# Gated linear attention and a channel mix on one core: gates taken two units ahead, masks placed per chunk, a new written order

## Chip, core and metric
One NeuronCore of a Trainium2 chip. The metric is device microseconds of one launch; lower is better. The profiled execution is one more launch, of which the profiler gives the span from the first to the last instruction.

## What is computed
Attention over 4 batches, 8 heads, 768 steps, head width 48, then a channel mix over 384 columns (mu_r and w_r are drawn eight times as large):

```python
f = 1.0 / (1.0 + np.exp(-f_logit))
for t in range(S):
    state = f[:, :, t, :, None] * state + np.einsum('bhd,bhe->bhde', k[:, :, t], v[:, :, t])
    y[:, :, t] = np.einsum('bhd,bhde->bhe', q[:, :, t], state)
x = y.transpose(0, 2, 1, 3).reshape(B, S, H * D)
x_prev = np.concatenate([zeros, x[:, :-1]], axis=1)
xk = mu_k * x + (1.0 - mu_k) * x_prev
xr = mu_r * x + (1.0 - mu_r) * x_prev
k = np.maximum(xk @ w_k, 0.0)
out = 1 / (1 + np.exp(-(xr @ w_r))) * (k * k @ w_v)
```

## The kernel before
**Tiling.** Time is cut into 24 chunks of 128 steps (six a batch); three chunks make a unit of 384 steps, eight units (u = 0 to 7) in all. Every unit passes through attention, chunk by chunk, and then through the mix.

**Attention, chunk i.** `b` is the running product of the gates (a DVE scan into PSUM), `bl` its last column; `ln` and `rb` on ACT give its reciprocal; `q`, `n`, `kr`, `k` scale the transposed queries and keys (DVE; `kr` on POOL). On PE, `TR` transposes k (4 matmuls), `S` forms the scores (32), `P` the chunk's sum of k and v (32), `YA` and `YB` the outputs (16 and 48). `kt` copies the transpose, `m` masks the scores, `zb`, `T`, `g`, `za` carry the state, `w` is a small copy between YA and YB, `y` writes the unit's input x, and three pairs of transfers `sp` spread two heads' rows over partitions (lines 189 to 365).

**Mix, unit u.** `d` and `xm` form the mixed inputs (0: for w_k, 1: for w_r), `xh` and `xl` split each into a high part in fp32r and the rest. `F` (8 blocks of 9 matmuls), `R` (3 of 9) and `W` (3 pairs of 12) multiply high x high, high x low and low x high. After F: `r` is the ReLU, `h` its square's high part, `kk` the square, `l` the square's low part. After R: `lg` is a copy and `sg` the sigmoid on ACT with its table load, and a load of the Exp table behind it. `o` is the product, `out` the store (lines 419 to 559).

**Weights** come as 64-bit words: 8 pieces of w_k, 4 of w_r, 6 of w_v. Each piece is loaded (`wk0`), turned into fp32 by three DVE steps (`wkS0`, `wkT0`, `wkX0`), and split by `wkH0` (ACT) and `wkL0` (POOL or DVE) (lines 561 to 603). `c` and `cm` load weights once more and reduce them for a range check; `lo`, `lot`, `lom`, `strong` turn that and the gates' least product into a flag, on which a general path (not taken here) hangs.

**Gates.** `f{u}` loads a unit's gate logits into one of three buffers. `sf{u}` is their sigmoid: units 0 to 2 have their own (line 387), and for unit 2 the Exp table is loaded behind it (line 389); unit u+3's is taken inside `sg{u}` (line 532).

**What sets the order.** Every instruction stands in one list written by hand, `ORDER` (lines 48 to 116); each engine's queue, SP's transfers among them, runs its words in the list's order and waits where data or a buffer isn't ready (lines 139 to 159, 700 to 713). A word's `/V`, `/A`, `/G` names the engine (DVE, ACT, POOL) where a task has a choice. A task's `after` list, its buffers and the list `chain` bound what an order may do: before, `chain` makes every F, R and W follow the one before it. PSUM gives four buffers `pm` that scans, transposes, weight steps and mix products share.

## Time and profile before
| | |
|---|---|
| median of 3 runs | 348.4 us (347.81 to 350.14) |
| the profiled execution's own time | 350.27 us |
| its span | 348.4 us |
| mean granted clock of TensorE | 0.981 |
| PE, DVE, ACT, POOL busy | 310.7, 253.7, 205.3, 168.0 us |
| transfers | 45.3 MB, 130 GB/s on the mean |

Busy time is the time in which an engine had an instruction in work; matmuls are pipelined, so a busy PE is not PE at its peak. A releaser (`<-`) is what ended an idle time. SPq is the queue that issues the transfers.

### The profile page before, as it was taken

To read this page: it belongs to the slowest core of one execution; us is meant where nothing else is said; L and a number is where in the kernel's file an instruction comes from. 1 tells how busy PE (TensorE), PEld (TensorE's weight loads), DVE (VectorE), ACT (ScalarE), POOL (GpSimd) and SP (SyncE) were. 2 spreads that over 40 slices of the span, in tenths; PEclk is the share of its full clock that TensorE was granted. 3 is DMA by queue.
4 is the path that set the end of the run, shared out by engine and by line. 5 is a ranking of instruction groups with operands and counts; after the bars stand their busy time and mean duration, and the time that the engine had idled before them with its cause. 6 is when DMAs were issued, how large, how long until landed. Compare 5 with 4: busy or idle time off the path is not lost.

```text
span 348.4 us, 10719 instructions
## 1 busy us (share of the span) xinstructions
PE 310.7 (89%) x4410; PEld 296.7 (85%) x4410; DVE 253.7 (73%) x521; ACT 205.3 (59%) x431; POOL 168.0 (48%) x209
## 2 busy tenths in 40 slices
...
GB/s 228 383 390 98 149 336 145 198 105 221 179 129 213 87 123 3 134 220 140 178 87 116 230 189 253 86 83 24 193 8 35 47 24 15 5 45 24 2 24 53
DMA packets 20649, 45.31 MB, mean 130 GB/s; under 512 B 2928, under 2 KB 13040, under 8 KB 20592
## 3 DMA queue, kind: packets, MB, share of 16 engines
...
q8 instruction: 36, 0.59, 0.7%
...
## 4 chain that ended last, share of the span: by engine, by line
PE 65%; DVE 15%; DMA 6%; issue 5%; ACT 3%; SPq 2%; POOL 2%; DVEq 0%; ACTq 0%; POOLq 0%
PE pm L468 55%; PE py L329 5%; DMA qk<-in_qkt 2%; PE pss L296 2%; DMA x<-stage 2%; PE pm L281 2%; DMA words<-in_wv 2%; DVE pm L590 1%; PE pss L316 1%; POOL k2l L505 1%; DVE pm L581 1%; DVE xm L445 1%; DVE pm L211 1%; DVE pm L428 1%; SPq L199 1%
## 5 line engine op out<-in xcount | busy, mean ns | idle before, releaser
L468 PE MATMUL pm<-xh,wk 128*128 128x384 f32 x384 | 105.7, 343 | 1.3 <-DVE words_k2l L593 0.6
L468 PE MATMUL pm<-wv,k2h 128*128 128x384 f32 x384 | 98.9, 339 | 0.8 <-DVE xm L445 0.8
L505 POOL TENSOR_TENSOR k2l<-kk,k2h 128x384 fp32r<-128x384 f32 x57 | 59.2, 1049 | 43.6 <-ACT k2h L495 25.6
L460 POOL TENSOR_TENSOR xl<-xm,xh 128x384 fp32r<-128x384 f32 x42 | 45.9, 1103 | 65.4 <-ACT xh L453 43.9
L468 PEld LDWEIGHTS pm<-xh,wk 128*128 128x128 f32 x384 | 70.0, 187 | 3.2 <-DVE words_k2l L593 0.8
L468 PEld LDWEIGHTS pm<-wv,k2h 128*128 128x128 f32 x384 | 68.7, 188 | 1.4 <-DVE xm L445 1.0
L468 PE MATMUL pm<-xl,wk 128*128 128x384 f32 x192 | 64.6, 337 | 0.0
L468 PE MATMUL pm<-wv,k2l 128*128 128x384 f32 x192 | 64.5, 336 | 0.0
L490 ACT ACTIVATE r<-pm 128x384 f32<-128x384 f32 x53 | 25.9, 491 | 32.2 <-PE pm L468 31.9
L468 PE MATMUL pm<-wr,xh 128*128 128x384 f32 x144 | 37.5, 341 | 1.9 <-DVE words L593 1.7
L211 DVE TENSOR_TENSOR_SCAN pm<-f,low 128x512 f32<-128x512 f32 x24 | 33.0, 1375 | 6.0 <-ACT ktk L285 3.7
L495 ACT ACTIVATE k2h<-r 128x384 fp32r<-128x384 f32 x64 | 32.8, 522 | 6.0 <-DVE r L491 4.6
L468 PEld LDWEIGHTS pm<-wv,k2l 128*128 128x128 f32 x192 | 36.1, 188 | 0.0
L468 PEld LDWEIGHTS pm<-xl,wk 128*128 128x128 f32 x192 | 36.1, 188 | 0.0
L497 DVE SCALAR_TENSOR_TENSOR kk<-pm,r 128x384 f32<-128x384 f32 x33 | 18.2, 555 | 19.3 <-ACT r L490 16.3
L555 DVE TENSOR_TENSOR o<-pm,lg 128x384 f32<-128x384 f32 x24 | 13.2, 551 | 24.6 <-PE pm L468 24.6
L281 PE MATMUL pm<-ident,qk 128*128 128x128 f32 x96 | 16.1, 294 | 16.2 <-DMA words_k2h<-in_wk 16.2
L229 POOL TENSOR_TENSOR qk<-qk,rb 128x256 f32<-128x256 f32 x21 | 16.3, 775 | 29.3 <-ACT bl L214 16.1
L329 PE MATMUL py<-qk,z 64*64 64x64 f32 x704 | 22.8, 235 | 8.4 <-ACT pm L437 7.0
L329 PEld LDWEIGHTS py<-qk,z 64*64 64x64 f32 x704 | 16.8, 140 | 14.8 <-ACT pm L437 7.2
L468 PEld LDWEIGHTS pm<-wr,xh 128*128 128x128 f32 x144 | 25.5, 188 | 2.6 <-DVE words L593 2.0
L281 PEld LDWEIGHTS pm<-ident,qk 128*128 128x128 f32 x96 | 12.2, 149 | 17.2 <-DVE qk L237 16.2
...
## 6 DMA issues: line engine op xcount, KB each, us to landing
...
```

Of the source, the lines that this page charges most:

```text
L211: pl.add(f"b{i}", ("V", lambda: nc.vector.tensor_tensor_scan(b().rearrange(FL), f().rearrange(FL), self.low.rearrange(FL), 1.0, op0=ALU.mu ...
L229: e.tensor_tensor(k()[:, ::2], k()[:, ::2], rb()[:, ::2], op=ALU.mult)
L281: nc.tensor.transpose(pk()[:, j], k()[:, j], self.ident)
L296: nc.tensor.matmul(self.pss[HALF[h], r, 64 * j : 64 * j + 64], k()[HALF[r], j, HALF[h]], q()[HALF[r], j, HALF[h ^ j % 2]], start=True, sto ...
L329: first[c, h] = nc.tensor.matmul(to, lhs, rhs, start=(c, h) not in first, stop=stop, skip_group_check=True)
L460: e.tensor_tensor(lo(), xm(), hi().bitcast(F32), op=ALU.subtract)
L468: nc.tensor.matmul(ps, lhs(a, j), rhs(bb, j), start=ends[0] and i == 0, stop=ends[1] and i == len(pr) - 1)
L490: pl.add(f"r{u}.{f}", ("A", lambda r=r, ps=ps: nc.scalar.activation(r(), ps(), AF.Relu)), ("V", lambda r=r, ps=ps: nc.vector.tensor_scalar ...
L495: pl.add(f"h{u}.{f}", ("A", lambda r=r, hi=hi: nc.scalar.activation(hi(), r(), AF.Square)), after=[f"r{u}.{f}"], **kw)
L497: pl.add(f"kk{u}.{f}", ("V", lambda r=r, ps=ps, kk=kk: nc.vector.scalar_tensor_tensor(kk(), ps(), 0.0, r(), op0=ALU.max, op1=ALU.mult)), ( ...
L505: e.tensor_tensor(lo(), kk(), hi().bitcast(F32), op=ALU.subtract)
L555: pl.add(f"o{u}.{t}", ("V", lambda t=t, ps=ps, o=o: nc.vector.tensor_tensor(o(), ps(), lg()[:, t], op=ALU.mult)), after=[f"W{u}.{t}1", f"s ...
```

## The change
- `AHEAD = 2`: the gates of unit u+2 (was u+3) are taken inside `sg{u}`; only units 0 and 1 have a sigmoid of their own. `b` of unit 2's chunks (6 to 8) now waits for `sg0`.
- The mask of every chunk is either one DVE step (`m/V`) or a copy by ACT (`m/A`) with a product on POOL (`mg/G`). Before, only chunk 0 had the second form; the new order gives it to chunks 0 to 5, 10, 13 to 18 and 20.
- `chain` is gone: F, R and W blocks of a unit may stand in any order, and among other units'.
- The mix's code is cut into functions (`add_inputs`, `add_square`) that could take a unit in parts; every unit is one part here, so names gain a 0 after the point (F0.02 is block 2 of unit 0) and sizes stay.
- `ORDER` is written anew. Parts moved between engines, before and after, as counts of words: `l` on POOL 57, 36, on DVE 7, 28; `xl` on POOL 42, 29, on DVE 6, 19; `za` on POOL 16, 10, on DVE 4, 10; `r` on DVE 11, 22; `kk` on DVE 33, 22; `xh` on DVE 23, 18; `lg` on DVE 4, 8.

```diff
@@ -28,8 +28,8 @@
 SIGMOID_SET = "sigmoid_and_others"
 EXP_SET = "natural_log_exp_and_others"
 LOW = 1.0e-18
-N, U = B * NCH, B * NU
-NQ, NFB = 4, 3
+N = B * NCH
+NQ, NFB, AHEAD = 4, 3, 2
 
 BUFS = {
     "pm": (4, [512]), "rb": (2, [NP, C]), "ss": (2, [2, NP, C // 2]), "ktk": (2, [NP, 2, D]), "v": (3, [H, D]),
@@ -41,78 +41,86 @@
 }
 
 
-AWAY = 1
-HALVED = 1
+UNITS = ((3,),) * (B * NU)
+FIRST = [sum(map(sum, UNITS[:u])) for u in range(len(UNITS) + 1)]
+U, FU = len(UNITS), N // UC
+HALVED = {0}
 
 
 ORDER = """
-f0.0 sf0.0 b0 bl0/V f0.1 sf0.1 b1 f0.2 sf0.2 f1 b2 wr0 wrS0 mu wrT0 wrX0 qk0 sf1 onemu b3 ex ln0 rb0 kr0/G q0 n0 bl1/A
-g2 ln1 qk1 q1 qk3 rb1 kr1/G q3 n1 ln3 rb3 bl3/A qk2 ln2 rb2 k0 cst k1 g1 n3 q2 kr3/G k3 TR0 S0 v0 kt0/A P0 TR1 bl2/A
-n2 m0 zb0/A wk0 wkS0 b4 YA0 w0/A kr2/G k2 S1 mg0 YB0 wkT0 ln4 kt1/A T0 za1/G g3 y0/A v1 m1 wkX0 P1 wk2 wr1 v2 TR2 wkS2
-rb4 kt2/A wv0 zb1 b5 T1 wvS0 wkT2 x00 YA1 wkH0 wrH0 bl4/A w1/A ln5 YB1 y1/A P2 wvT0 wkX2 wkH2 wv1 za2/G wrL0/G S2
-wkL2/G wkL0/G TR3 wvX0 kt3/A zb2 YA2 m2 S3 w2/A YB2 rb5 wrS1 wk6 wkS6 wrT1 wr2 f2 wkT6 wrX1 T2 za3/G wkX6 wvS1 wrS2
-qk4 kr4/G wvH0 wvL0/G wvT1 wrT2 v3 P3 y2/A qk5 kr5/G q4 wrX2 wvX1 sf2 wvH1 wvL1/G n4 m3 k4 g4 sp0.2 sp0.0 d0.00 xm0.00
-d0.12 zb3 YA3 d0.02 xm0.12 xm0.02 bl5/A xh0.00/A wk1 sp0.1 d0.01 wrH1 w3/A xh0.02/A S4 TR4 YB3 xl0.00/G wrL1/G xm0.01
-xl0.02/G xh0.01/A kt4/A wrH2 xl0.01/G wkS1 wk3 wkS3 d0.10 wkT1 wkT3 wkX1 wkH1 wkX3 wkH3 wkL1/G wkL3/G wrL2/G wk4 wk5
-wk7 wkS4 T3 wkT4 xm0.10 F0.0 wkH6 wkX4 y3/A x01 wkL6/G q5 n5 d0.11 xm0.11 k5 F0.1 wkS7 v5 r0.0/A kk0.0/A wv3 v6 v4 wr3
-h0.0 l0.0/G wkH4 r0.1/A kk0.1/A wkL4/G za4/G g5 wkS5 h0.1 l0.1/G F0.2 r0.2/A h0.2 wkT7 wv2 qk6 kk0.2/A l0.2/G wkT5
-wkX7 F0.3 r0.3/A wkX5 wkH5 wkL5/G wvS3 wrS3 wvT3 kk0.3/A h0.3 l0.3/G wkH7 xh0.10/A xl0.10/G P4 zb4 wvX3 wrT3 T4 za5/G
-wrX3 F0.4 r0.4/A TR5 YA4 xh0.11/A kk0.4/A kt5/A wvH3 F0.5 w4/A h0.4 m4 wrH3 wvS2 wkL7/V r0.5/A b6 wrL3/V xh0.12/A wvT2
...
-l7.5/G r7.6/A h7.6 kk7.6/V l7.6/G r7.7/A h7.7 kk7.7/V l7.7/G R7.0 R7.1 lg7.0/A R7.2 W7.00 W7.01 W7.10 W7.11 lg7.1/A
-lg7.2/A sg7 o7.0 out7.0 o7.1 W7.20 out7.1 W7.21 o7.2 out7.2
+wv0 f0.1 f0.0 f0.2 f1 wv1 qk1 qk0 qk2 wvS0 mu wvT0 v0 sf0.0 wvX0 sf0.1 cst b0 sf0.2 b1 wvH0 bl0/A sf1 b2 g1 wvS1 ex
+wvT1 bl1/A wvL0/V ln0 v1 ln1 wvX1 rb0 q1 wv2 rb1 kr0/G q0 n0 wk0 g2 k0 ln2 kr1/G qk3 bl2/A wk6 rb2 n1 S0 v2 q2 kr2/G
+wk4 TR0 k1 wk2 m0/A wvH1 n2 S1 kt0/A b3 wvL1/G P0 onemu wvS2 ln3 mg0/G TR1 zb0/A k2 m1/A YA0 wvT2 mg1/G kt1/A T0 w0/A
+wvX2 bl3/A rb3 YB0 za1/G q3 wvH2 kr3/G P1 qk4 wkS0 y0/A TR2 c7 zb1 wkS6 S2 g3 wkT0 wvL2/G YA1 m2/A n3 kt2/A wkT6 mg2/G
+wv3 T1 wkS4 wkX0 wkX6 w1/A b4 YB1 wkH6 wkL6/G P2 qk5 wkT4 bl4/A ln4 v3 k3 za2/G wk5 rb4 wkS2 wk7 y1/A kr4/G wkX4 zb2
+q4 wkH4 YA2 b5 w2/A YB2 T2 ln5 wkT2 wvS3 rb5 wkX2 kr5/G y2/A n4 TR3 q5 wkH2 za3/G S3 sp0.00 k4 bl5/A kt3/A g4 x00
+wkL4/G wvT3 wk1 TR4 n5 m3/A sp0.01 wkL2/G wkH0 wvX3 S4 kt4/A sp0.02 wkS5 wvH3 P3 cm7 d0.000 v4 wvL3/G wkT5 v5 d0.010
+c4 xm0.000 wk3 zb3 mg3/G xh0.000/A k5 wr2 YA3 m4/A c11 wkX5 TR5 d0.002 xl0.000/G xm0.010 d0.001 S5 xm0.002 w3/A wkH5
+wkL0/G xm0.001 xh0.002/A YB3 wkS1 xh0.001/A T3 d0.012 xl0.001/G xl0.002/V kt5/A za4/V P4 mg4/G y3/A wkT1 F0.02 zb4
+wkX1 xh0.010/A g5 cm4 wkL5/G m5/A xm0.012 wv5 F0.00 r0.02/A wr3 T4 mg5/G wkS3 kk0.02/A v6 wr0 d0.011 wrS2 wr1 YA4
+za5/G wkH1 wkT3 r0.00/A w4/V wkL1/G wkX3 YB4 kk0.00/A wrT2 wkH3 cm11 P5 xl0.010/G F0.04 y4/A zb5 c0 wrX2 f2 wkL3/G
+xm0.011 wrH2 f3 wvS5 xh0.011/A YA5 wrL2/G h0.00 wkS7 F0.05 w5/A xh0.012/A l0.00/G wkT7 h0.02 wvT5 r0.04/A l0.02/G YB5
+wvX5 kk0.04/A r0.05/A wkX7 F0.06 x01 xl0.011/G kk0.05/A wrS0 wkH7 wrT0 h0.04 xl0.012/G wrS1 wvH5 wrX0 F0.01 wrT1 y5/A
+wkL7/G wrX1 wrS3 wvL5/G wrH0 wrT3 F0.07 sp1.00 r0.01/A l0.04/V h0.05 wrX3 sp1.02 wrH1 wrL0/G r0.06/V wrH3 F0.03 wrL1/V
+kk0.01/A l0.05/G sp1.01 h0.01 wrL3/V h0.06 l0.01/G wv4 cm0 R0.0 qk8 r0.03/A qk6 kk0.06/A kk0.03/V c9 h0.03 l0.06/G
+d1.00 v7 r0.07/A R0.1 l0.03/G lg0.0/V kk0.07/A xm1.010 h0.07 R0.2 xm1.000 l0.07/G wvS4 xh1.000/A lg0.1/A wvT4 W0.20
+lg0.2/A d1.02 wvX4 xh1.010/V wvH4 d1.01 W0.10 sg0 wvL4/G xm1.011 xm1.002 xh1.002/V xl1.010/G c8 qk7 W0.11 xl1.000/G
+xm1.012 cm9 xl1.002/V c6 xm1.001 v8 W0.21 sf2 xh1.001/A b6 xl1.001/G W0.00 o0.1 ln6 b7 out0.1 rb6 bl6/V o0.2 ln7 W0.01
...
+kk6.05/A YB22 P23 y22/A F6.01 h6.05 R6.2 r6.01/A lg6.0/A kk6.01/V h6.06 zb23 h6.01 F6.07 lg6.2/A l6.01/G YA23 r6.07/V
+R6.1 w23/A kk6.06/V h6.07 m23/V l6.06/G cm10 lg6.1/A l6.05/G lo mg23/V YB23 kk6.07/A W6.00 sg6 y23/V l6.07/V sp7.00
+W6.01 sp7.02 sp7.01 d7.00 W6.10 xm7.010 xm7.000 xh7.010/A xh7.000/A xl7.010/G d7.01 W6.11 xl7.000/G o6.0 xm7.001
+out6.0 d7.02 xh7.001/A W6.20 xm7.012 xl7.001/G xm7.002 xh7.002/A xl7.002/G W6.21 F7.04 o6.2 o6.1 xm7.011 out6.1 F7.00
+r7.04/A xh7.011/V xl7.011/V F7.01 r7.00/V kk7.00/A h7.04 F7.07 h7.00 xh7.012/A l7.00/V kk7.04/A xl7.012/V l7.04/G
+F7.03 r7.07/A r7.01/A kk7.07/V h7.07 h7.01 F7.02 l7.07/G kk7.01/A F7.06 r7.02/A kk7.02/V R7.0 r7.06/A h7.02 l7.02/G
+F7.05 lg7.0/V r7.03/V kk7.03/A R7.1 h7.03 l7.03/G r7.05/V l7.01/V h7.05 R7.2 kk7.05/A h7.06 l7.05/G W7.10 lg7.2/A
+kk7.06/A lg7.1/A l7.06/G sg7 W7.00 W7.01 W7.11 o7.0 out7.0 out6.2 W7.20 o7.1 out7.1 lot W7.21 lom strong o7.2 out7.2
 """
...
-        if i < AWAY:
-            pl.add(f"m{i}", ("A", lambda: nc.scalar.copy(ss(), s4(self.pss[:, :, :256]))), after=I("S"),
-                   takes=[("ss", i)])
-            pl.add(f"mg{i}", ("G", lambda: nc.gpsimd.tensor_tensor(ss(), ss(), mask(), op=ALU.mult)),
-                   after=I("m"), uses=[("ss", i)])
-        else:
-            pl.add(f"m{i}", ("V", lambda: nc.vector.tensor_tensor(
-                ss(), s4(self.pss[:, :, :256]), mask(), op=ALU.mult)), after=I("S"), takes=[("ss", i)])
+        def masked():
+            nc.vector.tensor_tensor(ss(), s4(self.pss[:, :, :256]), mask(), op=ALU.mult)
+
+        pl.add(f"m{i}", ("V", masked), ("A", lambda: nc.scalar.copy(ss(), s4(self.pss[:, :, :256]))), after=I("S"),
+               takes=[("ss", i)])
+        pl.add(f"mg{i}", ("V", lambda: None), ("G", lambda: nc.gpsimd.tensor_tensor(ss(), ss(), mask(), op=ALU.mult)),
+               after=I("m"), uses=[("ss", i)])
...
+    def add_gates(self, pl, u):
...
-            if u < NFB:
-                def sf():
-                    nc.scalar.activation(t(), t(), AF.Sigmoid)
-                    if u == 2:
-                        nc.scalar.preload_act_table_set(EXP_SET)
-
-                pl.add(f"sf{u}", ("A", sf),
-                       after=[f"f{u}", "ex" if u > 1 else "sf0.2"])
+            if u < AHEAD:
+                pl.add(f"sf{u}", ("A", lambda: nc.scalar.activation(t(), t(), AF.Sigmoid)), after=[f"f{u}", "sf0.2"])
             else:
-                pl.add(f"sf{u}", ("A", lambda: None), after=[f"sg{u - NFB}"])
+                pl.add(f"sf{u}", ("A", lambda: None), after=[f"sg{self.turn(u)}"])
+
+    def turn(self, u):
+
+        return max(n for n in range(U) if FIRST[n] < UC * (u - AHEAD + 1))
...
-        chain = [f"W{u - 1}.{UC - 1}1"] if u > 0 and not alone else []
...
-            pl.add(f"F{u}.{f}", ("P", ff), after=chain + [f"xl{u}.0{j}" for j in range(KJ)]
-                   + ([] if alone else [f"wkL{f}"]),
-                   takes=[("pm", ("f", u, f))], uses=[("xh0", u), ("xl0", u)])
-            chain = [f"F{u}.{f}"]
...
-        more = not alone and u + NFB < U
+                   after=[f"R{u}.{t}"], **kw)
+        more = None if alone else next((w for w in range(AHEAD, FU) if self.turn(w) == u), None)
 
         def sig():
-            nc.scalar.activation(lg(), lg(), AF.Sigmoid)
+            nc.scalar.activation(lg()[:, :tiles], lg()[:, :tiles], AF.Sigmoid)
             if more:
-                t = self.f_t[u % NFB]
+                t = self.f_t[more % NFB]
                 nc.scalar.activation(t, t, AF.Sigmoid)
             if not alone and u < U - 1:
                 nc.scalar.preload_act_table_set(EXP_SET)
 
         pl.add(f"sg{u}", ("A", sig),
-               after=[f"lg{u}.{t}" for t in range(UC)] + ([f"f{u + NFB}"] if more else []) + (["ex"] if not alone else []),
+               after=[f"lg{u}.{t}" for t in range(tiles)] + ([f"f{more}"] if more else []) + (["ex"] if not alone else []),
                uses=[("lg", u)])
-        for t in range(UC):
+        for t in range(tiles):
             ps = lambda t=t: pm("v", u, t)[:, :DM]
...
                 pl.add(f"W{u}.{t}{h}", ("P", vp),
-                       after=chain + [f"l{u}.{f}" for f in range(NF // 2 * h, NF // 2 * (h + 1))]
+                       after=[f"l{u}.{of[t]}{f}" for f in range(NF // 2 * h, NF // 2 * (h + 1))] + [f"W{u}.{t}0"] * h
                        + ([] if alone else [f"wvL{p}" for p in range(3 * h, 3 * h + 3)]),
                        uses=[(f"k2h{h}", u), (f"k2l{h}", u)] + ([("pm", ("v", u, t))] if h else []),
                        takes=[] if h else [("pm", ("v", u, t))])
-                chain = [f"W{u}.{t}{h}"]
...
+    def add_inputs(self, pl, u, p, c, n, alone, halved):
+        nc = self.nc
+        x = lambda: self.b("x", u)
+        now, past = lambda j: x()[:, j, 1 + c : 1 + c + n], lambda j: x()[:, j, c : c + n]
+        xs = [] if alone else [("x", u)]
+        pm = lambda *key: self.b("pm", key)[:, :n]
+        own = lambda j: [] if alone else [f"sp{u}.{p}{j}"]
+        before = lambda j: [] if alone else [f"sp{u}.{p - 1}{j}" if p else f"x0{u}"]
...
+    def add_square(self, pl, u, f, p, c, n, mm3, alone):
+        nc = self.nc
+        h, fh = divmod(f, NF // 2)
+        key = (u, p, f)
+        name = f"{u}.{p}{f}"
+        ps = lambda: self.b("pm", ("f", *key))[:, :n]
+        xs = lambda a: self.b(("xh0", "xl0")[a], u)
+        ff = lambda: mm3(ps(), lambda a, j: self.w["wk"][a][:, j, f * P : f * P + P], lambda a, j: xs(a)[:, j, c : c + n],
+                         range(KJ))
+        pl.add(f"F{name}", ("P", ff), after=[f"xl{u}.{p}0{j}" for j in range(KJ)] + ([] if alone else [f"wkL{f}"]),
+               takes=[("pm", ("f", *key))], uses=[("xh0", u), ("xl0", u)])
...
```

## Rows read from the trace of the kernel before

**Rows 1.** Stretches of the profiled execution: its bounds and length in us, then busy time and instructions of PE, PE's weight loads, DVE, ACT and POOL, the granted clock, the DMA engines' share and GB/s; the last row sums all stretches.
```profile
10.00:20.00 10.00, 3.82 (x74) 3.07 (x74) 9.91 (x24) 7.82 (x16) 6.15 (x11) 1.00 1.05 374
20.00:30.00 10.00, 7.42 (x276) 6.07 (x276) 10.00 (x22) 7.28 (x23) 5.00 (x7) 1.00 0.87 329
30.00:40.00 10.00, 2.78 (x101) 2.62 (x100) 7.39 (x17) 6.64 (x10) 5.73 (x9) 0.75 0.14 37
40.00:50.00 10.00, 7.72 (x119) 6.81 (x120) 9.54 (x20) 9.31 (x25) 8.93 (x11) 0.74 0.92 293
50.00:60.00 10.00, 10.00 (x188) 9.10 (x187) 10.00 (x21) 9.39 (x23) 9.93 (x13) 1.00 0.53 214
60.00:70.00 10.00, 8.33 (x166) 7.73 (x165) 9.83 (x18) 7.52 (x20) 7.92 (x9) 1.00 0.59 179
...
120.00:130.00 10.00, 9.17 (x111) 9.02 (x100) 9.79 (x22) 3.42 (x8) 4.07 (x6) 1.00 0.51 156
...
170.00:180.00 10.00, 9.48 (x215) 8.76 (x213) 7.21 (x15) 6.75 (x18) 4.81 (x6) 1.00 0.52 186
...
sum 350.00, PE 310.73 PEld 296.69 DVE 253.71 ACT 205.33 POOL 168.03; mean PE 8.88 PEld 8.48 DVE 7.25 ACT 5.87 POOL 4.80
```
**Rows 2.** The chain of work that ended last, in order of time: start in us, length, what, and the count of merged instructions. L316 is P, L281 TR, L329 YA (x16) and YB (x48), L296 S, L468 the mix.
```profile
225.45 0.36 PE pss L316 x32
...
283.75 0.44 PE pm L281 x4
284.19 0.39 PE py L329 x16
284.58 0.47 PE pss L296 x32
285.05 0.72 PE py L329 x48
...
290.73 51.93 PE pm L468 x297
```
**Rows 3.** Instructions in order of time, PE at R0.0: start, length, engine, line, operation, output and inputs, count, and the idle time before it with what ended it.
```profile
64.50 0.62 PE L468 MATMUL pm<-wr,xh 128*128 128x384 f32 x2 [1.67 <-DVE words L593]
```
**Rows 4.** The same view, from 32 to 42 us: ACT at the sigmoid of load 2, and what DVE and PE waited for.
```profile
35.01 1.28 ACT L387 ACT_TABLE_LOAD   x1
36.31 1.48 ACT L387 ACTIVATE f<-f 128x1536 f32<-128x1536 f32 x1
37.81 1.28 ACT L389 ACT_TABLE_LOAD   x1
...
32.37 0.36 DVE L273 TENSOR_TENSOR sm<-pss,z 128x192 f32<-128x192 f32 x1 [1.20 <-PE pss L296]
40.27 0.61 DVE L440 SCALAR_TENSOR_TENSOR xm<-x,one_mu,pm 128x384 f32<-128x384 f32 x1 [1.68 <-ACT pm L437]
...
41.30 0.71 PE L329 MATMUL py<-qk,z 64*64 64x64 f32 x16 [7.05 <-ACT pm L437]
```
**Rows 5.** The same view, from 0 to 14 us: the first sigmoids, DVE's first steps and POOL's first product.
```profile
3.64 1.24 ACT L381 ACTIVATE f<-f 128x512 f32<-128x512 f32 x2 [1.61 <-DMA f<-in_zt]
...
4.30 1.23 DVE L211 TENSOR_TENSOR_SCAN pm<-f,low 128x512 f32<-128x512 f32 x1 [1.65 <-ACT f L381]
7.37 1.23 DVE L211 TENSOR_TENSOR_SCAN pm<-f,low 128x512 f32<-128x512 f32 x1 [0.50 <-ACT f L381]
9.58 0.46 DVE L581 TENSOR_SCALAR pm<-lg 128x288 int32<-128x288 int32 x1 [0.98 <-DMA lg<-in_wr]
...
12.96 0.72 POOL L229 TENSOR_TENSOR qk<-qk,rb 128x256 f32<-128x256 f32 x1 [11.82 <-ACT bl L214]
```
**Rows 6.** Groups of instructions by line: operation, output and inputs, shape, count, then busy us, mean ns of one, and idle time before them. In this order: sigmoid of a gate load inside sg, xl on DVE, l on DVE, one wv step, m on DVE, m on ACT, mg on POOL.
```profile
L532 ACT ACTIVATE f<-f 128x1536 f32<-128x1536 f32 x5 | 7.4, 1471 | 0.0
...
L460 DVE TENSOR_TENSOR xl<-xm,xh 128x384 fp32r<-128x384 f32 x6 | 4.6, 771 | 0.1
L505 DVE TENSOR_TENSOR k2l<-kk,k2h 128x384 fp32r<-128x384 f32 x7 | 4.6, 650 | 0.5 <-ACT k2h L495 0.5
L590 DVE SCALAR_TENSOR_TENSOR pm<-words,pm 128x512 int32<-128x512 int32 x6 | 4.1, 690 | 0.1
...
L308 DVE TENSOR_TENSOR ss<-pss,mask 128x512 f32<-128x512 f32 x23 | 15.7, 681 | 1.2 <-PE pss L316 0.8 <-PE pss L296 0.5
L303 ACT COPY ss<-pss 128x512 f32<-128x512 f32 x1 | 0.6, 586 | 0.8 <-PE pss L316 0.8
L305 POOL TENSOR_TENSOR ss<-ss,mask 128x512 f32<-128x512 f32 x1 | 2.3, 2300 | 0.7 <-ACT ss L303 0.7
```
**Rows 7.** Instructions in order of time again: the same DVE step twice, the second beside a POOL product.
```profile
128.22 0.55 DVE L460 TENSOR_TENSOR xl<-xm,xh 128x384 fp32r<-128x384 f32 x1
...
160.26 1.02 POOL L460 TENSOR_TENSOR xl<-xm,xh 128x384 fp32r<-128x384 f32 x1 [1.93 <-ACT xh L453]
160.33 1.36 DVE L460 TENSOR_TENSOR xl<-xm,xh 128x384 fp32r<-128x384 f32 x1
```
**Rows 8.** The six sp transfers of unit 7 as SP issued them (start, length of the issues), and the view of the DMA issues: count, size of one, median us from issue to landing.
```profile
292.25 3.68 SPq L417 DMA_DIRECT2D x<-stage  x6
...
x<-stage SPq DMA_DIRECT2D x48, 24.0 KB, 1.9
```

274 lines of the change are left out of this document (139 added, 135 removed).

## The prediction
> **What bounds the kernel now.** I read the stretches of ten microseconds first. PE is busy 310.7 of 348.4 us, and from 70 us on nearly all the time: the largest idle times there are 0.83 us in 120:130 and 0.52 in 170:180, and in all it is 272.65 to the last matmul less 310.7 - 40.1 of busy time, 2.0 [rows 1]. Before 70 us it is DVE that is full, 56.7 of the 60 us from 10 to 70, while PE has gaps of 7.2 us in 30:40, 2.3 in 40:50 and 1.7 in 60:70 [rows 1]. So the kernel is a start in which DVE (weights split into two parts, scans, the attention's products) decides when PE can run, and then 270 us of dense PE work. The chain of waits agrees: it ends in 297 matmuls in one piece, 51.93 us, 0.1748 us each [rows 2].
>
> That gives the measure that I use throughout: how late PE is, the time minus the PE work that the order puts ahead. A block of 9 matmuls (F, R) is 1.57 us, one of 12 (W) 2.10, a chunk of attention 0.44 + 0.47 + 0.36 + 0.39 + 0.72 = 2.38 [rows 2]. All work: 1368 x 0.1748 + 24 x 2.38 = 296.3 us. The last matmul ends at 342.65 [rows 2], so PE ends 46.3 us late; 5.7 us follow it. When the first receptance block R0.0 starts, at 64.50 [rows 3], 8 F (12.6) and 5.5 chunks (13.1) lie behind: 38.8 late. So 38.8 of the 46.3 arise in the start, and 7.5 after it: 2.0 as idle time, 5.5 as stretched starts where PE changes between kinds of blocks. No matmul is taken away, so the change can only win on these two sums.
>
> **The change part by part.** *Sigmoid of load 2.* It stood alone in the start: table load 1.28, sigmoid 1.48, table load 1.28 on ACT. Behind it PE waited 7.05 us and DVE 1.68 [rows 4]. Now it rides with sg0, which loads the tables anyway and takes 1.47 longer [rows 6]. What goes for the end is not 7.05: the next thing that PE would meet is DVE, which was at its limit all round it. DVE's 1.68 goes.
>
> The added wait: b6 now waits for sg0, thus for R0 and for some 5 us of ACT (two loads, unit 0's own sigmoid, 1.47). Queued behind b6 on DVE are all of chunks 6 to 8; F2 needs them, after W0 (12.6 us), F1 (12.6) and R1 (4.7) of PE work. That cover of 30 us is ample: 0. If it were gone, the price is the 5.
>
> *The first microseconds.* The first weight piece (wv0) is loaded ahead of the gates and split while the gates come. DVE waited 1.65, 0.50 and 0.98 us for transfers [rows 5]. Gates of 256 KB, loaded first, were there at 3.64 [rows 5], so 512 KB will be there at about 4.0 (estimate from that row and the 374 GB/s of 10:20 [rows 1]). DVE then starts at 4.0 instead of 4.30, and the 0.50 and 0.98 are filled. On SP the first products now stand behind 3.1 MB: 8.3 us at 374 GB/s and a start of 3, so 11.3, and DVE comes to them at about 12: 0, at most +1.
>
> *DVE's work ahead of R0.0*, counted word by word in both orders with each operation's mean: five more pieces of wv steps (5 x 0.69 = 3.4), three weight checks (1.9), five operations moved over from POOL and ACT (2.7, the low parts among them 0.77 and 0.65), one state sum and weight parts (0.9), less four masks (4 x 0.68 = 2.7) and one scan with its column (1.4): +4.9 [rows 6]. Neighbours overlap on DVE (busy 253.7 [rows 1] where counts times means give 278, a factor of 0.913), so +4.5. Against it stand the idle times that go: 0.30, 0.50, 0.98 and 1.68, and the 1.20 that a state sum waited at 32.37 [rows 4, 5], 4.7 in all. R0.0 comes at 64.5 + 4.5 - 4.7 = 64.3 plus new gaps X. X is at least 0, and at most 2.7: a wait like the 1.20 again, and 1.5 of collisions (four more exposed operations than before, at half the 0.8 that one lost [rows 7]). I take 1.4, the middle: 65.7. The new order has all of chunks 0 to 5 ahead of R0.0, half a chunk more (1.2). So PE is 65.7 - 12.6 - 14.3 = 38.8 late: **0**, from -1.4 to +1.3.
>
> *Masks.* m1 to m5 (and eight later ones) go to ACT and POOL: 0.68 of DVE becomes 0.59 on ACT and 2.30 on POOL, of which there is only one row [rows 6]. With them and other moves POOL's words ahead of R0.0 sum to 51.1 instead of 37.2 (five masks 11.5, two more wv parts 2.7). POOL's first product starts at 12.96 [rows 5], so 51.1 x 0.97 (its own overlap) ends at 62.5 without a gap, just ahead of DVE's 64.3. I cost it at 0; DVE hides it only while POOL's gaps stay under 1.8 us, or 3.2 with X.
>
> *Moves from POOL to DVE.* DVE's operations with both inputs in SBUF (low parts, state products) go from 23 to 64. A low part took DVE 0.55 at 128.22 and 1.36 at 160.33, begun 0.07 us after a POOL product of 1.02 [rows 7]. The means (0.771 and 0.650 [rows 6]) hold the collisions at before's density. The Trainium skill, "SBUF — State Buffer", section "Who interferes with whom", says that a DVE instruction with two SBUF inputs and a GpSimd one that reads SBUF exclude each other, and that whoever issues first holds the shared port pair for its whole length. The rows agree, since 1.36 is about the rest of the POOL product and 0.55. By that rule each of the 41 would wait half a POOL product (0.5) whenever POOL is busy, half of the time: some 10 us of DVE over the run, an estimate.
>
> After R0.0 DVE has room. With the same factor its words ahead of the first F of units 1, 2 and 3 (75.5, 126.3 and 149.7 us in the new order) let PE be 28.7, 35.7 and 22.4 late there; the old order's let it be 35.1, 28.9 and 32.3; and PE is 39 late or more by then. So DVE's total no longer decides, and of the 2.0 us of idle time I take 1.4 to go (bounds 0 and 2.0). The 5.5 stay: I count 128 changes of kind on PE from W0 on, against 122. The freed order of F, R and W by itself moves no work.
>
> *The end.* The check of the gates' size now runs between the last W blocks: two transposes on PE (half of the 0.44 for four [rows 2]) and four narrow DVE steps, each below the 0.69 of a full one [rows 6], beside W7.21's 2.1 us: +0.1, at most +0.8. Attention now runs up to just before W6, so unit 7's inputs come due: four steps of y (1.3), six transfers issued in 3.68 and the last landed 1.9 after its issue [rows 8], six DVE steps (3.7), one on ACT and one on POOL (1.6) make some 11.7 of the 12.6 us of W6. Margin 0.9: 0, at worst some 4.
>
> Sum: 0 - 1.4 + 0.1 = -1.3 on the profiled execution's span of 348.4, which is also the median of the runs (its own time was 350.27, 1.9 more around the span): **347.0**. About 1% (3.5 us) is what a measurement of this kernel can tell from no change.
>
> **Rivals.**
> *The start is really shorter.* X is 0 (-1.4), all 2.0 us of idle time goes, and half of the 5.5, as part of it is hidden waits (-2.7): 348.4 - 1.4 - 2.0 - 2.7 = 342.3. For it: the stalls of the start have named causes, which are removed [rows 4, 5], and DVE's sum allows it. Against it: DVE and POOL would both be at 95% or more, feeding each other without gaps.
> *POOL takes DVE's place (slower).* Place: the masks and low parts of chunks 0 to 5 on POOL, ahead of R0.0. POOL was idle some 11 of the 51.5 us from 12.96 to 64.5 [rows 1]; the new order leaves it 3.2. Each microsecond of gap beyond that delays low parts of weights and squares, and with them F, R and W, one for one. With 7.5 of the 11 kept R0.0 comes 4.3 later than forecast, and the waits after it don't go (1.0): 352.3. For it: POOL shows no such load in the start, and the mask's price rests on one row. Against: fuller queues leave fewer gaps.
> *Collisions decide (slower).* Six such steps and six scans stand ahead of R0.0 beside a nearly full POOL; half of them at the 0.8 lost at 160.33 [rows 7] is 4.8 instead of 0.7: 351.1. The skill's rule above would make it so, unless the order happens to keep the two engines apart.
> *It doesn't do what it says:* the order's other waits take the place of the removed ones, and the time stays: 348.4, inside the forecast's range.
>
> **How the numbers follow.** The forecast with the no-effect case 0.43; shorter start 0.33; POOL 0.14; collisions 0.06; the end's chain 0.04 (350 to 351). The range leaves a tenth on each side: 341.0 to 353.0; the forecast's own is 345.0 to 350.5. Faster by over 1% (under 344.9) 0.33; slower by over 1% (over 351.9) 0.21, which is two thirds of the slower cases and a tail of the forecast; within 1% 0.46.
>
> **What would show it.** Right: no table load on ACT between 12 us and R0.0; DVE busy from 4 us with no gap over 1 us until 60; R0.0 at 64 to 67; idle time of PE after 70 us under 1 us; PE's end 44 to 46 late. Wrong: R0.0 after 69 (POOL or collisions: POOL over 95% from 20 to 65, or DVE's low parts at means over 1.0) or before 63.5 (the shorter start); a gap of PE before F7.

## The result, and the profile after

| | before | after |
|---|---|---|
| median of 9 runs | 348.56 us (347.81 to 350.64) | 351.27 us (350.30 to 351.74) |
| ratio | | 1.0064, 95% interval 1.0039 to 1.0089 |
| profiled execution: own time, span | 350.27, 348.4 us | 351.26, 349.4 us |
| mean granted clock of TensorE | 0.981 | 0.963 |

The change is slower by 2 to 3 us, less than 1%. The forecast was 347.0; the time lies in its range (341 to 353) and on the other side of the time before.

The stretches of ten microseconds (columns as in [rows 1]) and the sum over all stretches:

```profile
10.00:20.00 10.00, 4.46 (x102) 3.92 (x103) 9.86 (x18) 6.83 (x13) 6.18 (x9) 1.00 1.01 360
20.00:30.00 10.00, 7.21 (x216) 6.02 (x214) 9.99 (x21) 5.67 (x16) 7.41 (x8) 0.67 0.79 261
30.00:40.00 10.00, 6.02 (x128) 4.68 (x124) 10.00 (x22) 7.57 (x22) 7.06 (x11) 0.50 0.54 170
40.00:50.00 10.00, 7.45 (x202) 6.62 (x195) 8.97 (x21) 8.21 (x20) 7.51 (x9) 0.67 0.80 242
50.00:60.00 10.00, 9.72 (x180) 8.63 (x180) 9.35 (x21) 8.61 (x22) 9.43 (x11) 0.96 0.88 287
60.00:70.00 10.00, 9.45 (x53) 8.74 (x52) 9.93 (x18) 8.07 (x21) 9.37 (x10) 1.00 0.58 201
...
sum 350.00, PE 317.35 PEld 301.04 DVE 263.85 ACT 209.50 POOL 144.60; mean PE 22.67 PEld 21.50 DVE 18.85 ACT 14.96 POOL 10.33
```

PE's large gap of 30:40 is gone, and PE is busy 6.6 us longer than before for the same matmuls. POOL is busy 6.2 to 9.4 of ten in the start, not at 95%. DVE is full but for 1.0 us in 40:50 and 0.65 in 50:60.

Instructions in order of time: DVE's first step, its one later gap over 1 us, PE at R0.0, at R0.1, and at the first F of unit 1:

```profile
4.84 0.69 DVE L613 TENSOR_SCALAR pm<-words 128x512 int32<-128x512 int32 x1 [2.19 <-DMA words<-in_wv]
...
45.19 1.14 DVE L535 SCALAR_TENSOR_TENSOR xm<-x,one_mu,pm 128x384 f32<-128x384 f32 x2 [1.03 <-ACT pm L532]
...
65.84 0.51 PE L453 MATMUL pm<-wr,xh 128*128 128x384 f32 x2
...
68.03 0.62 PE L453 MATMUL pm<-wr,xh 128*128 128x384 f32 x2 [0.44 <-DVE kk L582]
...
83.74 0.33 PE L453 MATMUL pm<-xh,wk 128*128 128x384 f32 x1
```

R0.0, 64.50 in [rows 3], starts at 65.84, where the forecast put it (65.7); in the five more profiles with the same start (e6, e12, e13, e16, e17 below) it comes at 66.30 to 66.76. The chain's last piece on PE (start, length), 342.66 in [rows 2], ends at 343.67:

```profile
341.57 2.10 PE pm L453 x12
```

PE is idle 0.6 us from 70 us to this end (273.67 less 273.05 of busy time), 2.0 before.

The kernel before was profiled twice more (e0 and e11 below). Both show R0.0 where [rows 3] has it, but not the largest wait of [rows 1], 0.83 us in 120:130, and they end about 1 us earlier. Rows of e11, a run of 349.06 us: R0.0, the first F of unit 1, the last piece of its chain, and the stretch 120:130.

```profile
64.44 0.62 PE L468 MATMUL pm<-wr,xh 128*128 128x384 f32 x2 [0.50 <-DVE words L593]
...
85.89 0.33 PE L468 MATMUL pm<-xh,wk 128*128 128x384 f32 x1
...
289.63 51.93 PE pm L468 x297
...
120.00:130.00 10.00, 10.00 (x128) 9.92 (x119) 9.64 (x21) 4.32 (x11) 4.07 (x7) 1.00 0.32 104
```

PE's lateness by the prediction's measure (time less the work ahead) tells where the time went. Ahead of the first F of unit 1 (F1) lie 8 F, 3 R, 6 W and seven chunks before (46.5 us), six chunks after (44.2).

| run | R0.0 | F1 | end | growth from F1 | growth from R0.0, less idle time |
|---|---|---|---|---|---|
| before, 350.27 | 38.8 | 39.4 | 46.3 | 6.9 | 5.5 |
| before, e11, 349.06 | 38.7 | 39.4 | 45.3 | 5.9 | 5.8 |
| after, 351.26 | 39.0 | 39.6 | 47.4 | 7.8 | 7.4 |

Against e11 the start costs 0.2 us and the stretch from F1 to the end 1.9, together 2.1 of the 2.2 between the two runs. The 0.2 is the least of six: in the five other profiles with the new start F1 comes 0.5 to 1.0 later than in after's. The growth from F1 is steady: 5.9 in three profiles of the old list (e0, e10, e11), 7.8 to 7.9 in three of the new one (after, e7, e8). But the old list has chunk 6 ahead of F1 and the new one behind it, so this growth sets 17 chunks against 18. From R0.0 on the work is the same but for half a chunk; there the growth less PE's idle time is 5.5 to 5.8 in five profiles of the old order (before, e0, e10, e11, e15) and 7.3 to 7.9 in four of the new (after, e7, e8, e17).

### The profile page after: what moved, and what is told of

Its sections match the earlier page's. It is cut to its first block, busy times and chain, and to the rows that moved or that the text cites. A ratio compares the mean times of both kernels' runs of the same rounds, so it can differ in the third digit from the quotient of the medians.

```text
span 349.4 us, 10686 instructions
## 1 busy us (share of the span) xinstructions
PE 317.4 (91%) x4410; PEld 301.0 (86%) x4410; DVE 263.8 (76%) x546; ACT 209.5 (60%) x446; POOL 144.6 (41%) x180
## 3 DMA queue, kind: packets, MB, share of 16 engines
q1 hardware_dynamic: 20592, 44.55, 38.8%
## 4 chain that ended last, share of the span: by engine, by line
PE 73%; DVE 11%; issue 4%; DMA 3%; ACT 3%; POOL 2%; SPq 2%; DVEq 0%; POOLq 0%; ACTq 0%
PE pm L453 62%; PE py L338 5%; DMA qk<-in_qkt 3%; PE pss L306 2%; PE pm L291 2%; PE pss L325 2%; DVE pm L622 1%; DVE pm L613 1%; DVE pm L221 1%; DMA x<-stage 1%; SPq L437 1%; POOL k2l L588 1%; DVE qk L247 1%; DVE xm L540 1%; DVE wr L632 1%
## 5 line engine op out<-in xcount | busy, mean ns | idle before, releaser
L453 PE MATMUL pm<-xh,wk 128*128 128x384 f32 x384 | 107.4, 346 | 0.1
L588 POOL TENSOR_TENSOR k2l<-kk,k2h 128x384 fp32r<-128x384 f32 x36 | 39.1, 1091 | 82.8 <-ACT k2h L580 32.4
L453 PEld LDWEIGHTS pm<-xh,wk 128*128 128x128 f32 x384 | 71.0, 190 | 1.9 <-DVE x L625 0.4
L555 POOL TENSOR_TENSOR xl<-xm,xh 128x384 fp32r<-128x384 f32 x29 | 31.4, 1092 | 48.4 <-ACT xh L548 24.1
L575 ACT ACTIVATE r<-pm 128x384 f32<-128x384 f32 x42 | 20.3, 489 | 27.2 <-PE pm L453 26.1
L306 PE MATMUL pss<-qk 64*64 64x64 f32 x768 | 18.7, 243 | 16.0 <-DVE qk L243 15.5
L306 PEld LDWEIGHTS pss<-qk 64*64 64x64 f32 x768 | 15.8, 154 | 18.5 <-DVE qk L243 15.5
L239 POOL TENSOR_TENSOR qk<-qk,rb 128x256 f32<-128x256 f32 x20 | 15.3, 767 | 28.3 <-ACT rb L229 15.6
L583 ACT ACTIVATE kk<-r 128x384 f32<-128x384 f32 x42 | 21.8, 522 | 8.0 <-DVE r L576 6.8
L540 DVE SCALAR_TENSOR_TENSOR xm<-pm,mu_sb,x 128x384 f32<-128x384 f32 x42 | 24.7, 610 | 2.3 <-POOL xl L555 1.9
```

Source lines behind the costliest of these rows:

```text
L239: e.tensor_tensor(k()[:, ::2], k()[:, ::2], rb()[:, ::2], op=ALU.mult)
L306: nc.tensor.matmul(self.pss[HALF[h], r, 64 * j : 64 * j + 64], k()[HALF[r], j, HALF[h]], q()[HALF[r], j, HALF[h ^ j % 2]], start=True, sto ...
L453: nc.tensor.matmul(ps, lhs(a, j), rhs(bb, j), start=ends[0] and i == 0, stop=ends[1] and i == len(pr) - 1)
L540: pl.add(f"xm{u}.{p}{w}{j}", ("V", lambda xm=xm, w=w, j=j: nc.vector.scalar_tensor_tensor(xm(), pm("d", u, p, j), self.mu_sb[:, w, j : j + ...
L555: e.tensor_tensor(lo(), xm(), hi().bitcast(F32), op=ALU.subtract)
L575: pl.add(f"r{name}", ("A", lambda: nc.scalar.activation(r(), ps(), AF.Relu)), ("V", lambda: nc.vector.tensor_scalar(r(), ps(), 0.0, None, ...
```

## The experiments

Theory A: the new start costs the time. Theory B: the new order behind it does, by dearer changes of kind on PE. Theory C is about what bounds the start of before. In the diffs, lists are cut to the words that move. Where a time is given as so much over after, the two are of different series: the kernel before's median was 347.8 to 349.4 us in them, so about 1 us of such a difference can be the series.

**e0 and e11: the kernel before again.** No edit.

> The kernel before, unchanged, timed and profiled once more. Its nine runs so far lie in two groups, six from 347.8 to 348.6 and three from 350.1 to 350.6, and the profiled execution (350.27) was of the upper one; the kernel after has one group, 350.3 to 351.7. Theory 1 (the upper group is a longer span, and the difference arises in the start): this kernel's runs at 348.3 have spans near 346.4, and a profile of one shows R0.0 some 2 us ahead of 64.5, the rest as before. Theory 2 (it lies around the span): spans are 348.4 in both groups, and R0.0 is at 64.5 in every profile.

> The kernel before once more, one profile, for what its runs of 347 have that those of 350 have not. Theory 1 (the wait times behind the start differ from run to run): R0.0 at 64.5 to 64.7 again and an end between 340 and 343 by its waits over 0.25 us after 72 (1.74 us in the run of 350.3, 0.71 in that of 349.1). Theory 2 (the start differs): R0.0 under 64.

e0: 348.48 us (347.10 to 351.19, 12 runs), ratio 0.9986 (0.9956 to 1.0017). There are no two groups, but a spread of 4 us; each run's span is 1.8 us shorter than its time. R0.0 is at 64.65 and 64.44, so what differs between these profiles arises behind the start: PE's waits over 0.25 us after 72 are 1.69, 0.83 and 0.73 us in before, e0 and e11. The profile on which the forecast was built was of a run 1.7 us above the median.

**e1, e4, e2, e5: halves of the two lists.**

```diff
-ORDER = before[:R0.0] + before[R0.0:]
+ORDER = before[:R0.0] + after[R0.0:]    # e1; e4: cut at F1.0
+ORDER = after[:R0.0] + before[R0.0:]    # e2; e5: cut at F1.0
```

> The list of before up to R0.0 (with unit 2's own sigmoid and its table loads, but without chunk 6's first words), then the list of after, with the words that after has ahead of R0.0 and before has not put in behind it. Theory A (the new start is what costs the time): 348 to 349, ratio near 1.000. Theory B (the new order behind R0.0 costs it, by more changes of kind on PE): 350.5 to 351.5, ratio near 1.006. If both share it, near 1.003.

> The list of before up to the first F of unit 1 (with unit 2's own sigmoid in the start), then the list of after; the weight checks that after has ahead of this point stand one by one behind it, and chunk 6 stays where before has it. The point lies behind unit 0's W blocks, so that no wait for the sigmoid of unit 0 is at the seam. Theory B (behind this point the new list has more dear changes of kind on PE: summed by the medians of each pair of neighbours in the traces, 14.0 us against 12.1): 350.0 to 350.6, ratio 1.004 to 1.006. Theory A (the start of the new list costs it): 348.5, ratio 1.000.

> The list of after up to R0.0, then the list of before; the sigmoids of loads 2 and 3 are both taken with unit 0's, and chunk 6's and 7's gate products stand behind it. Theory A (new start): 350.5 to 352, ratio near 1.007. Theory B (the rest): 348 to 349, ratio near 1.000. Chunks 6 and 7 come later than in before, which has 9 us of PE work as cover; a gap of PE ahead of their transposes would show if that is not enough.

> The reverse: the list of after up to the first F of unit 1, then the list of before, chunk 6's products on PE behind three F blocks; loads 2 and 3 share unit 0's sigmoid. Theory A (start): 350.5 to 351.5, ratio 1.006 to 1.008. Theory B (the rest): 348.6 to 349.0, ratio 1.000 to 1.001; the 0.6 us that the start is late in the profile stays.

388.8, 391.1, 362.5 and 358.3 us. PE's longest wait was 15.8 us in e1, 25.2 in e4 and 9.1 in e2; in e5 it waited 4.9 us in several pieces behind F1. Halves of two lists do not fit each other: loads, PSUM buffers and DVE's queue were laid out for the other half. None tells A from B.

**e3 and e14: the gates' part alone.**

```diff
-... wvX1 sf2 wvH1 ...  b6 ln6 q6 ... F0.6 F0.7 R0.0 ...
+... wvX1 wvH1 ... F0.6 F0.7 R0.0 ... sg0 b6 ln6 q6 ... o0.0 ... F1.2 TR6 ... TR7
+# e14: sg0 o0.0 d1.2 xm1.02 o0.1 b6 ...
```

> The list of before with one change: unit 2's own sigmoid and table load are gone from the start and taken with unit 0's (together with load 3's), and chunk 6's and 7's gate products stand behind it. Mine of the prediction (DVE's 1.68 us of idle time goes and PE's end comes earlier by that much): 346.7, ratio near 0.995, R0.0 near 62.8 in a profile that would else have it at 64.5. Rival (DVE or another wait is next and takes the room): 348.3 to 348.6, ratio 1.000. Rival (the two chunks' wait for the sigmoid reaches PE): 349.5 to 351, with a gap of PE between 75 and 95 us.

> Once more the list of before with unit 2's sigmoid taken with unit 0's, but with unit 0's first products out (o0.0, o0.1) ahead of chunk 6's gate product on DVE, so that the PSUM buffers come free in time; chunk 6 stands behind the first three F of unit 1, chunk 7 behind it. In e3 R0.0 came at 63.85, 0.8 us earlier than in before. Mine of the prediction for this part alone (-1.7): 347.2. From e3's start (-0.8), if nothing is lost behind it: 348.2 to 348.6. Rival (attention comes some 20 us later in the stretch of unit 1, and PE's pieces there wait or stand at dearer places): 350 or more, with the growth of PE's lateness from F1 to the end above the 11.8 us of before.

362.56 and 360.58 us: both slower. The start is what they show. PE's wait of 7.05 us in [rows 4] is still there without the sigmoid; from e3 (YA3), then e14 (YA3 and R0.0):

```profile
41.33 0.71 PE L338 MATMUL py<-qk,z 64*64 64x64 f32 x16 [6.17 <-DVE z L277]
```
```profile
39.16 0.70 PE L338 MATMUL py<-qk,z 64*64 64x64 f32 x16 [6.17 <-ACT bl L224]
...
61.80 0.51 PE L453 MATMUL pm<-wr,xh 128*128 128x384 f32 x2
```

R0.0 came at 63.85 in e3 and 61.80 in e14, from one list up to that point; e3's granted clock was 0.55 in 25:30, e14's 1.00. So the sigmoid's removal, with chunk 6's gate product gone from ahead of R0.0 too, is worth 0.6 to 2.8 us at R0.0 in the old list, and one profile cannot say it closer. All of it is given back: with chunks 6 and 7 behind sg0, e14 is 39.3 late at F1, as before, and 10.4 us later than before at F2 (136.36 against 125.96; PE waits 2.2 us for kk, 2.0 for o, 1.8 for xl, all queued on DVE).

**e7 and e8: one part of the start taken back in the new list.**

```diff
-... wv3 ... bl5/A ... f2 ... sf2 b6 ...
+... wv3 f2 ... sf2 bl5/A ... b6 ...            # e7, sf2 with its own table loads
-m1/A mg1/G ... m5/A mg5/G
+m1/V ... m5/V                                  # e8
```

> The list of after with unit 2's sigmoid back in the start, with its two table loads (4 us of ACT) ahead of chunk 5's last column, its gates loaded earlier. Mine of the prediction (only DVE's idle time of 1.7 us is what such a stall costs): R0.0 near 67.5, 353.0, ratio 1.012. Rival (the whole 4 us on ACT are passed on, since DVE has no more slack): R0.0 near 70, 355.3, ratio 1.019. Rival (other waits of the start cover it): 351.3, ratio 1.007.

> The list of after with the masks of chunks 1 to 5 as one DVE step each, as in before, in place of ACT's copy and POOL's product. Mine of the prediction (DVE is what bounds the start: five steps of 0.68 us come back, times 0.913, 3.1 us): R0.0 at 68.9 and 354.4, ratio 1.016. Rival (the detour over ACT and POOL lies on the chain to YB and costs as much as DVE saves): 351.3, R0.0 at 65.8. Rival (POOL is the worse of the two): 350.0.

e7: 354.01 us (353.07 to 355.41), 2.7 over after. Rows of e7: ACT at the sigmoid, PE at chunk 4's scores and at R0.0.

```profile
37.85 1.28 ACT L397 ACT_TABLE_LOAD   x1
39.15 1.48 ACT L397 ACTIVATE f<-f 128x1536 f32<-128x1536 f32 x1
40.65 1.28 ACT L399 ACT_TABLE_LOAD   x1
...
43.03 1.14 PE L306 MATMUL pss<-qk 64*64 64x64 f32 x32 [3.05 <-ACT ss L315]
...
69.17 0.51 PE L458 MATMUL pm<-wr,xh 128*128 128x384 f32 x2
```

R0.0 comes 2.4 to 3.3 us later than in the six profiles of lists equal to after's up to there (65.84 to 66.76), not DVE's 1.7: ACT now copies the masks, so chunk 3's copy stands behind the sigmoid and PE waits for it. In the new list the removed sigmoid is worth what it costs ACT; the new list spends it elsewhere.

e8: 352.79 us (352.21 to 353.38), 1.5 over after, half of what I expected; by the intervals of their ratios (1.0069 to 1.0134 and 1.0039 to 1.0089) it cannot be told from after. R0.0 at 66.67 lies within those six. So five steps taken off DVE move R0.0 by less than a profile's scatter.

**e10 and e15: the start of the old list.**

```diff
-... q4 wrX2 wvX1 sf2 ... sp0.2 sp0.0 ... wk1 sp0.1 ... wk3 ...
+... wk1 wk3 qk5 kr5/G q4 wrX2 wvX1 sf2 ...     # e10 and e15
-m1 m2 m3 m4
+m1/A mg1/G ... m4/A mg4/G                      # e15 only
```

> The list of before with the loads of two pieces of w_k (1 and 3) moved ahead of unit 0's spread transfers on the transfer queue, nothing else. In e3, with the sigmoid and its table loads gone, the output piece YA3 still started at 41.33 (41.32 with them), and the chain of waits there ran over six issues of spread transfers at 0.6 us to the load of w_k's piece 1, landed at 43.5. Theory C (what bound the start of before was the transfer queue behind the spread transfers, not the sigmoid): R0.0 1.5 to 2.5 us earlier, near 62.6, and 346.5, ratio 0.994. Rival (DVE's sum of work bounds it, and the wait only moves): R0.0 at 64.5, 348.6, ratio 1.000.

> The list of before with the two loads of w_k ahead of the spread transfers (as in e10) and the masks of chunks 1 to 4 by ACT and POOL instead of DVE, as after has them. If DVE's sum of work bounds the start of before: 4 x 0.68 x 0.913 = 2.5 us less of it, R0.0 at 61.5 to 62 and 346.5, faster than both. Rival (in before's order the detour over ACT and POOL delays the pieces behind it by as much, as e8 says of after, where five masks were worth 0.8 us): R0.0 at 63.3 to 64, 348.6 to 349.

e10: 349.55 us, ratio 1.0008 (0.9986 to 1.0029), R0.0 at 63.94: no gain in time, theory C fell. e15: 351.51 us, ratio 1.0094 (1.0061 to 1.0128), R0.0 at 67.29. Four masks less on DVE made the start 3.3 us longer than e10's: DVE then waited 2.8 us for ACT, 2.3 and 1.1 for sums and scores of PE, and 1.4 for POOL. Its sum of work alone does not bound the start; by these waits the chain through each chunk does as well.

**e6, e9, e17: PE's pieces joined or parted, in one list.**

```diff
-... P11 YA10 S11 YB10 F2.02 YA11 R2.0 YB11 ...
+... YA10 P11 S11 YB10 F2.02 R2.0 YA11 YB11 ...   # e6, 33 pieces of after
-... F1.2 TR7 F1.3 S7 ... YA11 S12 P12 YB11 R2.0
+... F1.2 F1.3 TR7 S7 ... YA11 R2.0 S12 P12 YB11  # e9, 33 pieces of before
-... F4.02 F4.03 TR17 YA16 ... W5.01 TR22 YA21
+... F4.02 TR17 F4.03 YA16 ... TR22 W5.01 YA21     # e17, four of after
```

> The list of after with 33 pieces of PE moved by at most 1.7 us of work, behind the first F of unit 1, so that attention's pieces stand together and transposes are followed by a mix block where they can be: nothing else is changed. The sum of the changes of kind by pair medians falls from 14.0 to 12.3. Theory B: 1.7 us faster than after, 349.6, ratio to before 1.003. Rival (the moved pieces are needed sooner by DVE and ACT, and PE waits for what they make): no gain, 351.3 or more, with idle time of PE above 0.6 us after 70.

> The list of before with PE's pieces behind the first F of unit 1 shifted by one mix block at most, so that the sum of the changes of kind by pair medians rises from 12.1 to 14.5 us, as high as in after (14.0); attention's pieces keep their order, and none comes more than 0.55 us earlier. Theory B (these pairs are what the new list pays behind its start): 2.4 us slower than before, 351.0, ratio 1.007, idle time of PE after 70 not above before's 0.7 to 2.0. Rival (the pairs' cost is hidden or made up by waits that go): 348.6, ratio 1.000.

> The list of after with four transposes (chunks 6, 17, 20 and 22) one mix block earlier, where k was ready 2.5 us or more ahead of them, so that no new wait comes: two of them then stand alone between mix blocks or end a group. Theory B: 0.2 to 0.45 us less growth of PE's lateness from F1 to the end, 13.55 to 13.8 against 14.01 in the profile; in time 351.0, not to be told from after. Rival (the price is a wait that moves along): 14.0.

e6: 353.71 us, 2.4 slower than after where 1.7 faster was expected. Each of five YA put next to its YB meets the small copy between them, and YB starts 0.75 us after YA. From e6:

```profile
140.66 0.46 PE L338 MATMUL py<-qk,z 64*64 64x64 f32 x16
141.41 0.46 PE L338 MATMUL py<-qk,z 64*64 64x64 f32 x16 [0.28 <-ACT done L356]
```

Behind a YA without such a wait the next piece starts after 0.28 us (in e6 from 141.41, where YB begins with 16 matmuls of YA's kind, to its next at 141.69), so the pair loses 0.47; parting it by a mix block, as after does seven times and before twice, costs a change of kind instead. e9: 360.29 us, with waits of 6.2 us. e17: 351.42 us, and from F1 to the end 7.9 us of growth instead of 7.8. No run lowered the growth. None of the three isolates the price.

**e12, e13, e16: the price of a change of kind by itself.**

```diff
+def spare():                                    # e12, e13: eight 64x64 products
+    for j in range(4):
+        for r in (0, 1):
+            nc.tensor.matmul(self.py[HALF[r ^ j % 2], r, n : n + 64], self.ident[HALF[r], HALF[j % 2]], ...)
+            # e16 instead: four of nc.tensor.transpose(self.py[:, j % 2, 320:448], self.ident, self.ident)
-F7.04 ... F7.00 ... F7.01 ...
+F7.04 z0 ... F7.00 z1 ... F7.01 z2 ...          # e12, e16: twelve places
+F7.04 ... F7.00 ... F7.01 z0 z1 z2 z3 ...       # e13: three places
```

> The list of after with twelve idle products added on PE: each is eight 64x64 fp32 matmuls of the identity into a part of PSUM that nothing reads, like one output piece YA, one behind each of twelve mix blocks of unit 7 (from F7.04 to W7.10), where attention is over and nothing waits for them. With e13 it measures what a change of kind costs by itself. Theory B (a mix block and the piece behind it lose 0.11 us, the piece and the mix block behind it 0.11 more, as the pair medians say, without any wait): 12 x 0.28 of work and 12 x 0.22 of changes, 6.0 us over after: 357.3; 2.0 us over e13. Rival (those 0.1 us are waits for data, not the price of the change): 354.7, and no difference from e13.

> The same twelve idle products, in three heaps of four behind F7.01, F7.06 and R7.2. Theory B: 12 x 0.28 of work and 3 x 0.22 of changes, 4.0 us over after: 355.3. Rival: 354.7, as e12.

> As e12, but each of the twelve idle pieces is four 128x128 transposes, as TR has them. Not counting transposes that stand alone between two mix blocks, the old list has 22 places behind the first F of unit 1 where attention's pieces part two mix blocks, the new one 28; six more at the 0.34 us that e12 less e13 gives are 2.0 of the 2.2. That holds if lone transposes are free of the price, as the pair medians say (0.01 ahead of one, 0.004 behind it). Theory B so: 12 x 0.35 of work and nothing more, 4.2 us over after, 355.5; each mix block with the piece behind it takes 1.94 us in the profile. Rival (every change of kind costs 0.34): 12 x 0.69, 359.5, and 2.28 us each; then the count of such places, 35 and 36, cannot be the cause.

358.68, 355.65 and 356.86 us: 7.4, 4.4 and 5.6 over after. From F7.04 to W7.00 PE takes 19.46 us in after, 26.30 in e12, 23.24 in e13 and 24.57 in e16. e12 less e13 is 3.06 us for nine places, **0.34 us each** (3.03 by the runs), where 0.22 was expected; a lone group of transposes takes 0.43 in all, 0.08 more than was expected for its work. Nobody waits for these products and they wait for nobody. PE's weight loads show the price; from e12, then e16:

```profile
317.33 0.19 PEld L454 LDWEIGHTS pm<-xh,wk 128*128 128x128 f32 x1
317.77 0.33 PEld L701 LDWEIGHTS py<-ident 64*64 64x64 f32 x16 [0.25 <-issue]
318.16 0.19 PEld L454 LDWEIGHTS pm<-xh,wk 128*128 128x128 f32 x1
```
```profile
317.72 0.19 PEld L454 LDWEIGHTS pm<-xh,wk 128*128 128x128 f32 x1
317.90 0.53 PEld L699 LDWEIGHTS py<-ident 128*128 128x128 f32 x4
```

The first 64x64 weights behind a mix block come after 0.25 us of "issue", in which the engine waits for nothing that the profile shows; 128x128 transposes follow without a gap.

## Why the prediction was wrong

**The step that failed** is the one behind R0.0: "of the 2.0 us of idle time I take 1.4 to go ... The 5.5 stay: I count 128 changes of kind on PE from W0 on, against 122." The idle time did go, from 2.0 to 0.6. But growth from R0.0 to the end is 8.4 (39.0 to 47.4), 0.4 of it R0.1's wait and 0.6 idle: 7.4 of stretched starts where I kept 5.5. Counting all changes alike hid what they cost. Leaving out places where only transposes stand between two mix blocks, attention parts the mix 26 times from R0.0 on in the old list and 29 times in the new one: three more at 0.34 are 1.0 us of the 1.9 that are missing (1.6 against e11). Behind F1 the counts are 23 and 29, but three of the old list's 26 are chunks 5 and 6 ahead of F1.

The traces have the same 1.0 at these places. From the last mix matmul ahead of a place to the first one behind it, less idle time and less the lengths that the prediction's sum gives to the pieces, the 26 places take 3.3 to 3.4 us too long in before, e0, e10 and e11, and the 29 take 4.3 to 4.6 in after, e7, e8 and e17. Two of the new places are YA11 and YB11, which the old list had in one group; their weight loads in after:

```profile
138.23 0.33 PEld L338 LDWEIGHTS py<-qk,z 64*64 64x64 f32 x16 [0.25 <-issue]
...
140.40 0.32 PEld L338 LDWEIGHTS py<-qk,z 64*64 64x64 f32 x16 [0.25 <-issue]
```

The sums of the weight loads agree. Groups by line from R0.0 to the end (columns as in [rows 6]; idle time last), first after (65.8 to 344), then e11 (64.4 to 342):

```profile
L338 PEld LDWEIGHTS py<-qk,z 64*64 64x64 f32 x528 | 11.7, 133 | 4.8 <-issue 3.6 <-DVE kk L582 0.2 <-ACT bl L224 0.2
...
L306 PEld LDWEIGHTS pss<-qk 64*64 64x64 f32 x576 | 10.1, 135 | 1.4 <-issue 0.8 <-DVE sm L283 0.6
L291 PEld LDWEIGHTS pm<-ident,qk 128*128 128x128 f32 x72 | 8.7, 140 | 0.7
L325 PEld LDWEIGHTS pss<-v,ktk 64*48 64x48 f32 x528 | 7.8, 121 | 1.3 <-issue 0.9 <-ACT k2h L580 0.2
```
```profile
L329 PEld LDWEIGHTS py<-qk,z 64*64 64x64 f32 x560 | 12.3, 133 | 4.9 <-issue 3.4 <-ACT r L490 0.4 <-DVE ss L308 0.3
...
L296 PEld LDWEIGHTS pss<-qk 64*64 64x64 f32 x576 | 10.2, 135 | 0.7 <-issue 0.5 <-DVE ss L308 0.2
L281 PEld LDWEIGHTS pm<-ident,qk 128*128 128x128 f32 x72 | 8.7, 140 | 0.9 <-DVE qk L237 0.2
L316 PEld LDWEIGHTS pss<-v,ktk 64*48 64x48 f32 x528 | 7.9, 121 | 0.8 <-issue 0.5 <-ACT k2h L495 0.2
```

Ahead of attention's weights the loads sit idle 8.2 us after and 7.3 before, and the whole 0.9 of the difference is "issue" (5.3 against 4.4). So the price is shown, and about half of the 1.9 is paid at these places; where the other half arises is not shown. Nor does the count alone forecast a list: e6 has 25 such places, four fewer than after, and its growth from R0.0 less idle time is 7.7, no lower. The three runs that moved pieces in the lists brought other waits or gained nothing.

**The profile that was read.** 1.1 of the 2.0 us of idle time was in that run alone (0.9 and 0.8 in e0 and e11), and the median run has 1.7 us less. I saw the execution's own time beside the median and took the change from its span all the same. A gain read off such waits was not there to be had in most runs.

**Sigmoid of load 2** (DVE's 1.68): wrong in size and reason. PE's wait was not the sigmoid's (6.17 without it in e3 and e14). The part is worth 0.6 to 2.8 at R0.0 in the old list and 2.7 in the time of the new one, since ACT carries the masks there.

**b6's wait, at 0:** right here; k6 was ready 3.6 us ahead of TR6 (88.50). e3 and e14 show how much that hung on the rest of the order.

**The first microseconds:** DVE began at 4.84, not 4.0; the first weight piece landed later than the estimate.

**DVE's work ahead of R0.0:** the sum came out (65.7 against 65.84, lateness 38.8 against 39.0), but its terms are in doubt and five other profiles with this start have R0.0 up to 0.9 us later, so that it came out this closely is in part luck. Masks counted 0.62 each; e8 found five of them within the scatter of R0.0, and e15's four cost 3.3 where 2.5 were to be gained. Two slips of addition change nothing: the terms of the +4.9 make 4.8, and 348.4 less 1.3 is 347.1.

**POOL** did not take DVE's place: it was 62 to 94% busy in the stretches from 10 to 70. The mask's price of 2.30 from one row was too high; the mean of 14 is 1.36.

**Collisions:** low parts on DVE and masks on POOL in the profile after (columns as in [rows 6]):

```profile
L588 DVE TENSOR_TENSOR k2l<-kk,k2h 128x384 fp32r<-128x384 f32 x28 | 18.0, 649 | 3.9 <-ACT k2h L580 3.5
...
L555 DVE TENSOR_TENSOR xl<-xm,xh 128x384 fp32r<-128x384 f32 x19 | 10.6, 562 | 2.1 <-ACT xh L548 2.0
L317 POOL TENSOR_TENSOR ss<-ss,mask 128x512 f32<-128x512 f32 x14 | 19.0, 1357 | 8.5 <-ACT ss L315 8.4
```

The two means fell, from 0.771 and 0.650 to 0.562 and 0.649; against medians of 0.549 and 0.558 all 47 low parts lost 2.8 us. By the rule of the Trainium skill, "SBUF — State Buffer", section "Who interferes with whom", my estimate had been 10 us over the run. A few steps collided (the longest 1.25 us), which agrees with it, but most took the 0.55 of a step that meets no POOL product.

**The end:** right. PE has no gap ahead of F7 or behind it, and 5.7 us follow the last matmul, as before.

Of the rivals the shorter start fell (R0.0 was not earlier), and so did POOL, the end's chain and the unchanged time. Collisions had forecast 351.1, next to the measured time, but by 4.1 us more at R0.0, which did not come: that number is a coincidence. None named dearer changes of kind. Of the prediction's signs of being right two failed: DVE has one gap of 1.03 us, and PE ends 47.4 late instead of 44 to 46.
